# Squares of the first two blocks moved inside SBUF, and their scaling placed two output products earlier, in a fused attention and MLP kernel

## The chip, the cores and the metric

The kernel runs on one core of one Trainium2 chip. The metric is device time in microseconds (us), the median of three runs: 485.56 us (485.5 to 487.13).

The engines are named as in the profile: PE is TensorE's matrix multiplication and PEld its weight loads, DVE is VectorE, ACT is ScalarE, POOL is GpSimd and SP is SyncE, which here only issues DMA transfers. DMA transfers are issued by SP or by POOL, each in the order in which its instructions were written.

## The reference

```python
def _A_ref(x, wqkv, wo):                       # linear attention, 32 heads of 16
    q, k, v = ...                              # from x @ wqkv
    phi = lambda t: where(t > 0, t + 1, exp(t)) + 1e-6
    pq, pk = phi(q), phi(k)
    kv = einsum("bhsd,bhse->bhde", pk, v)
    z = einsum("bhsd->bhd", pk)
    num = einsum("bhqd,bhde->bhqe", pq, kv)
    den = einsum("bhqd,bhd->bhq", pq, z)[..., None] + 1e-6
    return (num / den) @ wo

def _B_ref(x, w1, b1, w2):                     # Dense, Mish, Dense
    h = x @ w1 + b1
    return (h * tanh(softplus(h))) @ w2

mod = (silu(c) @ w_mod).reshape(1, 6, 1, -1)   # sa, ca, ga, sb, cb, gb
h = layernorm(x) * (1 + ca) + sa
x = x + ga * _A_ref(h, wqkv, wo)
h = layernorm(x) * (1 + cb) + sb
x = x + gb * _B_ref(h, w1, b1, w2)
```

x is 2048 x 512, wqkv 512 x 1536, wo 512 x 512, w1 512 x 1792 and w2 1792 x 512, all in float32.

## The kernel before, in words

**Tiles.** The 2048 rows are four blocks of 512 rows, a block is four tiles of 128 rows. Most SBUF tiles are 128 x 512 float32 (2 KB in each partition) and come from one pool of `SLOTS` = 95 equal slots (tag "T"); a new tile takes a slot that an earlier one has given back. Each operand of a product is split into an upper part (rounded to fp32r, on ACT, line 82) and the rest (on DVE, line 88), and a product is three matmuls (lines 72 to 76). Part of the MLP's products are done by a Strassen-like scheme with seven products of sums in place of eight (`product`, line 1189).

**Order.** The order on each engine is the order in which the program issues its instructions (`manual_schedule`). Side work is written as Python generators: `spawn` queues one, and `tick` (line 57) lets every running one issue its next piece. So a statement "one tick later" says where in each engine's order the instructions stand. An engine that waits for an operand holds up all that stands behind it.

**The stage around the change.** After the query products, the loop of line 1338 issues the attention output products `o_unit` of blocks 1 to 3, counted by n = 4 b + t from 4 to 15; `o_unit` is twelve matmuls on PE (line 938). Beside it run, by ticks:

- `attend(3)` (line 878), spawned at n = 5. For block 3 it forms the denominators, sends their reciprocals to DRAM (line 890) and loads them spread over the partitions in four transfers `rd` (line 894), both on SP. After three ticks it multiplies the query tiles by them (DVE, line 902), two at the tick of n = 9 and two at that of n = 10. The splits follow: `qs_..h` on ACT, `qs_..l` on DVE one tick later. The product of n = 12, block 3's first, is the first that needs them.
- `norm_first(b, t)` (line 951) for blocks 0 and 1. It normalizes the finished rows (ACT, line 208) and turns each tile in 32 x 32 squares into a wide tile (DVE, line 239; the tag "W" has a single buffer). After a block's fourth tile the squares go to DRAM, `spread` on SP (line 245, four transfers of 256 KB, each from 32 partitions). Then four transfers bring them back (line 252, SP) as tiles with features along the partitions. For block 0 this last step is two ticks later (`WAIT = (2, 0)`), at n = 7.
- `turned_f(b, j)` (line 1025) scales such a tile on ACT (line 256, `hf_n`). The dictionary `turn_at` (line 1337) sets when. Block 0 is scaled at n = 10 (tiles 0 and 2) and n = 11 (tiles 1 and 3), each followed by a `split_b`. Block 1 is scaled at n = 13.

**Behind it.** At n = 13 `pairs_begin` (line 1208) starts the MLP's first products with block 0's split tiles (b11). `columns_early(0)` (line 1046) then makes the sums t1 to t4 of blocks 0 and 1 on DVE (line 1054) and splits them. `two_pairs` (line 1272) runs the products of the first two pairs with them; for them it calls `pair_first` of the second pair (a12 times b21) ahead of everything else. Its last step but one is the first product with w2 (`d_unit`, lines 74 to 76, tile `oacc`), which needs the split of w2's first tile. `w2_job` (line 707) makes that; `WAITS` (line 1382) says after how many ticks each of the first three starts.

**Late in the kernel** `load_r` (line 1418) loads rows of block 2 or 3 into a tile of its own tag "Y" (4 KB in each partition, one buffer).

Of the kernel before, what the change touches and what calls it, by code (L numbers as in the profile page):

```python
# [8 lines left out]
F32 = mybir.dt.float32  # L9
# [4 lines left out]
P = 128  # L14
# [3 lines left out]
NB = S // 512  # L18
NF = F // P
LAG = 3  # L20
SLOTS = 95
EPS = 1e-5
TINY = 1e-6

# [1 line left out]
def block_kernel(ctx: ExitStack, tc: tile.TileContext, x, wqkv, wo, w1, b1t, w2, c, wmodt, out):  # L26
    nc = tc.nc
    act, dve, pool, pe, sp = nc.scalar, nc.vector, nc.gpsimd, nc.tensor, nc.sync

    cst = ctx.enter_context(tc.tile_pool(name="cst", bufs=1))  # L30
    big = ctx.enter_context(tc.tile_pool(name="big", bufs=1))
# [6 lines left out]
    def sb(name, dt=F32, shape=(P, 512)):  # L38

        return big.tile(list(shape), dt, tag="T", name=name, bufs=SLOTS)  # L40

# [8 lines left out]
    def spawn(gen):  # L50
        fresh.append(iter(gen))
# [58 lines left out]
    c0 = sb("c0")  # L110
# [73 lines left out]
    def ln_stats(key, b, j, t):  # L184

        for d, name, shape in (mv, "mv", [P, 4, 2]), (rs, "rs", [P, 4]), (nb, "nb", [P, 4]):
            if (key, b) not in d:
                d[key, b] = cst.tile(shape, F32, tag=name, name=f"{name}_{key}_{b}", bufs=NB)
        st6 = cst.tile([P, 6], F32, tag="st6", name=f"st6_{key}_{b}_{j}", bufs=4)
        dve.bn_stats(st6, t)  # L190
        dve.bn_aggr(mv[key, b][:, j, :], st6)
# [4 lines left out]
    def ln_rstd(key, b, lo=0, hi=4):  # L196

        y = rs[key, b][:, lo:hi]
        pool.tensor_tensor(y, y, half[:, lo:hi], op=ALU.pow)  # L199
# [33 lines left out]
    wide, squares, turned = {}, {}, {}  # L233
# [7 lines left out]
    def spread(key, b, eng=sp):  # L241
        d = drp.tile([16, 32, 4, P], F32, name=f"sq_{key}_{b}")
        w = wide.pop((key, b))
        for a in range(4):
            eng.dma_start(bass.AP(tensor=d.tensor, offset=d.offset + P * a, ap=[[D, 32], [32 * D, 16], [1, P]]),
                          w[32 * a:32 * (a + 1)].rearrange("p m t c -> p m (t c)"))
        squares[key, b] = d

    def load_squares(key, b, j, eng=sp):
        d = squares[key, b]  # L250
        v = turned[key, b, j] = sb(f"sq_{key}_{b}_{j}")
        eng.dma_start(v, bass.AP(tensor=d.tensor, offset=d.offset + P * D * j, ap=[[D, P], [1, D]]))
# [689 lines left out]
    def later_sums(b, t):  # L942

        s_, v = first_sums.pop((b, t)), xt["r", b, t]
        if ("n", b) not in rs:
            for d, name in (rs, "rs"), (nb, "nb"):
                d["n", b] = cst.tile([P, 4], F32, tag=name, name=f"{name}_n_{b}", bufs=NB)
        act.activation(sb(f"scrap_n_{b}_{t}"), v, AF.Square, scale=-1.0 * D, bias=s_[:, 0:1], accum_out=s_[:, 1:2])
        return s_

    def norm_first(b, t):

        if (b, t) in SEEDED:
            if b:
                yield
            s_ = later_sums(b, t)
            yield
            dve.tensor_scalar(rs["n", b][:, t:t + 1], s_[:, 1:2], 1.0 / D ** 3, EPS, op0=ALU.mult, op1=ALU.add)
            ln_rstd("n", b, t, t + 1)
            yield  # L960
            dve.scalar_tensor_tensor(nb["n", b][:, t:t + 1], s_[:, 0:1], -1.0 / D, rs["n", b][:, t:t + 1],
                                     op0=ALU.mult, op1=ALU.mult)
        elif b and t > 1:
            ln_stats("n", b, t, xt["r", b, t])
            ln_eps("n", b, t, t + 1)
            ln_rstd("n", b, t, t + 1)
            yield
            ln_shift("n", b, t, t + 1)
        else:
            if b:  # L970
                yield
            sums = act_sums("n", b, t, xt["r", b, t])
            yield
            sums_eps("n", b, t, sums)
            yield
            sums_shift("n", b, t, sums)
        v = sb(f"n_{b}_{t}")
        ln_apply("n", b, t, xt["r", b, t], v, act)
        yield
        turn("n", b, t, v)  # L980
        if t == 3:
            yield
            spread("n", b)
            for _ in range(WAIT[b]):
                yield
            for j in (0, 2, 1, 3):
                load_squares("n", b, j)

    SEEDED = [(0, 0), (0, 1), (0, 2), (0, 3), (1, 0), (1, 1)]
    SEEDS = [(0, 0), (0, 1), (0, 2), (0, 3), (), (), (1, 0), (1, 1)]  # L990
# [4 lines left out]
            if i:  # L995
                o_seed(*i)

    WAIT = (2, 0)

    def norm_tile(b, t):  # L1000

# [27 lines left out]
    def split_b(b, j, name):  # L1029
        return split(f"{name}_{b}_{j}", hf[b, j], op_b, (name, j % 2))  # L1030
# [15 lines left out]
    def columns_early(c0):  # L1046

        b11, b12, b21, b22 = [[hf.pop((b, c + h)) for c in range(2)] for h in (0, 2) for b in (c0, c0 + 1)]
        t = [[sb(f"t_{c0}_{c}_{i}") for i in range(4)] for c in range(2)]
        todo = {}  # L1050

        def diff(c, i):
            u, v = ((b12[c], b11[c]), (b22[c], t[c][0]), (b22[c], b12[c]), (b21[c], t[c][1]))[i]
            dve.tensor_tensor(t[c][i], u, v, op=ALU.subtract)

        def upper(name, c, v):
            todo[name, c] = split(f"{name}_{c0}_{c}", v, op_b, (name, c))
            next(todo[name, c])

        for c in range(2):  # L1060
            diff(c, 0)
            diff(c, 1)
            upper("t2", c, t[c][1])
        for c in range(2):
            upper("t1", c, t[c][0])
        yield
        for name in "t2", "t1":
            for c in range(2):
                run(todo[name, c])
        for c in range(2):  # L1070
            diff(c, 2)
            upper("t3", c, t[c][2])
        yield
        for c in range(2):
            run(todo["t3", c])
            diff(c, 3)
        yield
        for name, v in ("t4", [t[c][3] for c in range(2)]), ("b22", b22):
            for c in range(2):
                upper(name, c, v[c])  # L1080
        yield
        for name in "t4", "b22":
            for c in range(2):
                run(todo[name, c])
# [145 lines left out]
    def pair_first(c0, g, p11):  # L1230
        m = mish(product(g, "a12", "b21", onto=p11), c0, 2 * g)
        next(m)
        spawn(m)
# [37 lines left out]

    def two_pairs(c0, g0, g1, begun, between):

        if c0 == 0:
            pair_first(c0, g1, begun[1][1])
        s0 = pair_early(c0, g0, begun[0], "h")
        tick()
        pc = product(g1, "s1", "t1", "h")
        pair_middle(g0, *s0)
        tick()  # L1280
        pa, p11 = begun[1]
        if c0:
            pair_first(c0, g1, p11)
        u2 = sb(f"u2_{g1}")
        product(g1, "s2", "t2", onto=pa)
        act.activation(u2, pa, AF.Copy)
        tick()
        pair_end(c0, g0, *s0, step=False)
        between[0]()
        pair_middle(g1, pa, pc, u2)  # L1290
        tick()
        between[1]()
        tick()
        pair_end(c0, g1, pa, pc, u2)
# [39 lines left out]
            load_wb(6)  # L1334


    turn_at = {10: [(0, 0), (0, 2)], 11: [(0, 1), (0, 3)], 13: [(1, 0), (1, 2), (1, 1), (1, 3)]}
    for b in range(1, NB):
        for t in range(4):
            n = 4 * b + t  # L1340
            if n == 13:
                begun = pairs_begin(("h", "tp"))
            for i, j in turn_at.get(n, ()):
                turned_f(i, j)
                if not i:
                    spawn(split_b(i, j, f"b{j // 2 + 1}1"))
            seed_next()
            if t == 3 and b == NB - 1:
                spawn(rows(2, 3))
            o_unit(b, t)  # L1350
            if n == 13:
                spawn(columns_early(0))
            if b == 1:
                spawn(norm_first(1, t))
            if n == 11:
                for f in range(4):
                    load_w2(f)
            if n == 5:
                spawn(attend(3, 3, sp))
            tick()  # L1360
# [18 lines left out]
            yield  # L1379
        yield from gen  # L1380

    WAITS = {0: 1, 1: 2, 2: 2}
    JOBS = {1: (0, 1, 2), 2: (3, 4), 3: (5, 6), 4: (7, 8), 5: (9, 10), 6: (11, 12, 13)}
    for g in range(1, G):
        for f in JOBS[g]:
            spawn(after(WAITS.get(f, 0), w2_job(f)))
        if g + 1 < G:
# [21 lines left out]
    banks, rq, U = {}, {}, {}  # L1409
# [8 lines left out]

    def load_r(n, c):

        y = rq[n, c] = big.tile([P, 16, 64], F32, tag="Y", name=f"rq_{n}_{c}", bufs=1)
        for a, d in enumerate(in_squares(x1d[L + n], c)):
            sp.dma_start(y[32 * a:32 * (a + 1)], d)

# [39 lines left out]
    rn, V, Z = {}, {}, []  # L1464
# [63 lines left out]
    for n, g in enumerate(pairs):  # L1528
# [20 lines left out]
        if n == 0:  # L1549
            begun = [pair_begin(L, pairs[i], ("tp" if i else "h", "acc")) for i in range(2)]  # L1550
# [16 lines left out]
    for k, (name, n) in enumerate(units[:4 * G]):  # L1567
        for _ in range(2 if k in (6, 10, 14, 18) else 1):
            if ahead_of:
                nm, m = ahead_of.pop(0)  # L1570
                spawn(left_prep(nm, pairs[m]))
        for _ in range(2 if k < 3 else 1):
            if loads:
                nm, m = loads.pop(0)
# [14 lines left out]
    for t in range(4):  # L1589
        p = last[t][:, 0:D // 2]  # L1590
# [3 lines left out]
        v = rn[t // 2][:, t % 2, :]  # L1594
# [35 lines left out]
```

## Time and profile before

| what | before |
|---|---|
| median of three runs | 485.56 us (485.5 to 487.13) |
| the profiled execution | 488.12 us, span 486.4 us |
| granted TensorE clock, mean | 0.995 |
| PE busy | 478.1 us, 98% |
| DVE busy | 393.9 us, 81% |
| ACT busy | 309.4 us, 64% |
| POOL busy | 119.8 us, 25% |
| DMA | 89.10 MB, mean 183 GB/s |
| HBM read and written | 59.52 MB and 27.00 MB |

The span goes from the first to the last instruction of one profiled execution; the execution is 1.72 us longer than that. A row of the timeline gives start and length in us, engine, source line, operation, output tile <- input tiles, how many it stands for, and in brackets how long the engine had been idle before it and whose result ended that. The times are from the start of the span. "SPq" is SP's queue of DMA issues; such a row shows how long the issue took, not the transfer. Rows that stand for several instructions ("x2") give the time from the first's start to the last's end. The view by stages gives the busy time (and the number of instructions) of PE, PEld, DVE, ACT and POOL in a stretch, then the granted TensorE clock, the share of the 16 DMA engines' time in use, and GB/s.

### The profile page before, as it was taken

The page shows a single profiled execution, that of the slowest core. Times are in us where ns is not written, and L with a number is a line of the kernel's source. Part 1 is how long each engine was busy: PE and PEld are TensorE (multiplying, and loading weights), DVE is VectorE, ACT ScalarE, POOL GpSimd, SP SyncE. Part 2 cuts the span into 40 slices and gives each one's busy share as a digit, 9 for nine tenths or more (in the row PEclk, how much of TensorE's full clock was granted, in tenths as well). Part 3 has the DMA queues.
Part 4 walks back from the last instruction along what each step waited for, and adds up shares of the span by engine and source line. Part 5 has one row for each costly group of instructions (what it writes and reads, how often), then busy time and mean ns, then how long its engine had stood idle before and what let it go on. Part 6 is the DMA issues. An engine that isn't in the chain of part 4 may idle for free.

```text
span 486.4 us, 7005 instructions
## 1 busy us (share of the span) xinstructions
PE 478.1 (98%) x2290; PEld 390.3 (80%) x2290; DVE 393.9 (81%) x785; ACT 309.4 (64%) x555; POOL 119.8 (25%) x200
## 2 busy tenths in 40 slices
PE   8999999999999997999999999999999999999997
PEld 7688877768887886787888888888888888888887
DVE  6899898998899797699689883699635687779992
ACT  5886468756666974778777765695265677547600
POOL 3673121000022211102223524343111101354400
PEclk9999999999999999899999999999999999999999
DMA  8904859543865349868439849989553502486964
GB/s 301 385 7 89 193 113 282 178 141 109 261 186 130 103 108 259 266 206 238 144 97 276 262 126 280 395 286 314 153 156 87 119 12 86 109 216 157 233 160 102
DMA packets 86399, 89.10 MB, mean 183 GB/s; under 512 B 22961, under 2 KB 59321, under 8 KB 86362
## 3 DMA queue, kind: packets, MB, share of 16 engines
q1 hardware_dynamic: 61320, 53.37, 36.9%
q0 software_dynamic: 22784, 34.49, 25.9%
q10 hardware_dynamic: 2258, 0.79, 0.7%
q8 instruction: 18, 0.29, 0.2%
q14 instruction: 19, 0.16, 0.1%
HBM read 59.52 MB, written 27.00 MB: 178 GB/s over the span
## 4 chain that ended last, share of the span: by engine, by line
PE 73%; DVE 9%; DMA 8%; ACT 5%; issue 2%; SPq 1%; POOL 1%; DVEq 0%
PE p_a L1195 14%; PE p_s L1195 7%; PE oacc L75 5%; PE oacc L76 5%; PE oacc L74 5%; PE m L76 5%; PE m L74 5%; PE m L75 5%; PE p L1195 3%; DMA sq_x<-wide_x 2%; PE pq_a L376 2%; PE o L938 2%; PE gacc L75 1%; PE pq L74 1%; DMA rd<-rden_d 1%
## 5 line engine op out<-in xcount | busy, mean ns | idle before, releaser
L1200 DVE TENSOR_TENSOR cb<-p_s,u 128x512 f32<-128x512 f32 x28 | 19.2, 688 | 10.7 <-ACT u L1248 10.7
L777 POOL DMA_DIRECT2D wb<-w2d x14 | 9.8, 705 | 64.6 <-issue 23.5
L1187 ACT ACTIVATE ub<-cb,b1c 128x512 f32<-128x512 f32 x28 | 20.0, 718 | 7.0 <-DVE cb L1200 6.8
L199 POOL TENSOR_TENSOR rs_n<-rs_n,half 128x1 f32<-128x1 f32 x16 | 9.7, 608 | 45.5 <-DVE rs_n L225 19.8
L1526 POOL DMA_DIRECT2D wt_m<-w2t x20 | 14.0, 702 | 25.3 <-DVE cb L1200 12.4
L1205 ACT ACTIVATE p<-p_a 128x512 f32<-128x512 f32 x12 | 7.0, 582 | 20.6 <-PE p_a L1195 12.2
L1162 ACT ACTIVATE u<-p,b1c 128x512 f32<-128x512 f32 x14 | 9.6, 686 | 13.3 <-PE p L1195 13.3
L1248 ACT ACTIVATE u<-p_a 128x512 f32<-128x512 f32 x14 | 8.4, 598 | 14.1 <-PE p_a L1195 13.9
L890 POOL DMA_DIRECT2D rden_d<-rden x2 | 1.5, 736 | 60.0 <-DVE rden L888 60.0
L256 ACT ACTIVATE hf_n<-sq_n,mc 128x512 f32<-128x512 f32 x16 | 12.3, 806 | 5.6 <-DMA sq_n<-sq_n 5.4
L1162 ACT ACTIVATE u<-p_a,b1c 128x512 f32<-128x512 f32 x14 | 9.6, 686 | 8.6 <-PE p_a L1195 8.5
L783 POOL DMA_DIRECT2D w2b<-w2d x20 | 10.6, 542 | 15.5 <-PE oacc L76 6.1
L290 DVE SCALAR_TENSOR_TENSOR ku<-e_k,relu_k 128x512 f32<-128x512 f32 x16 | 11.0, 685 | 2.0 <-ACT relu_k L288 2.0
L902 DVE SCALAR_TENSOR_TENSOR q<-q,rd 128x512 f32<-128x512 f32 x16 | 10.5, 685 | 1.7 <-DMA rd<-rden_d 1.7
L290 DVE SCALAR_TENSOR_TENSOR q<-e_q,relu_q 128x512 f32<-128x512 f32 x16 | 10.7, 690 | 1.4 <-ACT relu_q L288 1.4
L199 POOL TENSOR_TENSOR rs_x<-rs_x,half 128x1 f32<-128x1 f32 (+1 forms) x10 | 7.8, 785 | 15.7 <-DVE rs_x L194 14.9
L190 DVE BATCH_NORM_STATS2 st_x<-x 128x6 f32<-128x512 f32 x13 | 8.8, 677 | 2.9 <-DMA x<-in_x_dram 2.9
L287 ACT ACTIVATE e_k<-pk 128x512 f32<-128x512 f32 x16 | 9.5, 591 | 2.6 <-PE pk L76 2.6
L929 POOL DMA_DIRECT2D x1d<-r x8 | 4.4, 547 | 27.2 <-DVE r L924 27.2
L299 POOL DMA_DIRECT2D ku<-ku x8 | 7.2, 940 | 13.8 <-DVE ku L290 13.8
L175 DVE SCALAR_TENSOR_TENSOR wm<-wm,sc_row 128x512 f32<-128x512 f32 x16 | 10.5, 687 | 0.0
L716 DVE TENSOR_TENSOR w2g<-w2r,gb_bc 128x256 f32<-128x256 f32 x28 | 10.0, 420 | 0.0
(1611 smaller groups left out, 1883.5 us busy)
## 6 DMA issues: line engine op xcount, KB each, us to landing
wm<-in_wmodt_dram SPq DMA_DIRECT2D x24, 256.0 KB, 4.4
w1p<-in_w_dram SPq DMA_DIRECT2D x24, 256.0 KB, 6.4
w2b<-w2d POOLq DMA_DIRECT2D x20, 256.0 KB, 6.8
wt_m<-w2t POOLq DMA_DIRECT2D x20, 256.0 KB, 3.6
r<-in_x_dram SPq DMA_DIRECT2D x16, 256.0 KB, 3.0
sq_n<-wide_n SPq DMA_DIRECT2D x16, 256.0 KB, 3.7
sq_n<-sq_n SPq DMA_DIRECT2D x16, 256.0 KB, 6.7
x<-in_x_dram SPq DMA_DIRECT2D x15, 256.0 KB, 4.9
```

The lines of the kernel that those rows point to most:

```text
L74: pe.matmul(o, st[0], mv[0], start=start, stop=False)
L75: pe.matmul(o, st[0], mv[1], start=False, stop=False)
L76: pe.matmul(o, st[1], mv[0], start=False, stop=stop)
L199: pool.tensor_tensor(y, y, half[:, lo:hi], op=ALU.pow)
L256: act.activation(dst.rearrange("p (t a i) -> p t a i", t=4, a=4), turned.pop((key, b, j)).rearrange("p (a t i) -> p t a i", a=4, t=4), AF. ...
L290: dve.scalar_tensor_tensor(dst, e, 1.0, r, op0=ALU.min, op1=ALU.add)
L783: pool.dma_start(w2s[f][i], w2d[f // 2, i][:, f % 2, :])
L1162: act.activation(u, p, AF.Mish, bias=b1c[:, f:f + 1])
L1187: act.activation(u, p, AF.Mish, bias=b1c[:, f:f + 1])
L1195: pe.matmul(p, st, mv, start=onto is None and c == 0 and i == 0, stop=c == 1 and i == 2, skip_group_check=onto is not None)
L1200: dve.tensor_tensor(out, p, u, op=ALU.add)
L1526: pool.dma_start(v, w2t[g][:, :, SUM[name], :])
```

## The change

It has five parts.

1. `move_squares` replaces `spread` and `load_squares` for blocks 0 and 1. The wide tile goes straight into a second SBUF tile `V` (8 KB in each partition, one buffer, used by both blocks in turn) in 16 transfers of 64 KB, each from 32 partitions to 32 partitions, 512 bytes at a time. They are issued alternately by SP and POOL, at the place where `spread` stood. The two ticks of wait for block 0 are dropped.
2. The scaling of block 0 is issued at n = 8 and n = 9 in place of 10 and 11. Its four splits are issued at n = 11, behind that product.
3. In `two_pairs` the second pair's first product is issued at its later place (behind the first pair's third sum product) for the first call too.
4. `WAITS`: the first `w2_job` starts without a wait (1 tick before), the third after 3 ticks (2 before).
5. The slots of tag "T" are 93 in place of 95, and `load_r` uses half of a tile of tag "V" in place of "Y".

```diff
-SLOTS = 95
+SLOTS = 93
@@
+    def move_squares(key, b, queues):
+
+        w = wide.pop((key, b))
+        v = big.tile([P, 4, 4, P], F32, tag="V", name=f"sq_{key}_{b}", bufs=1)
+        n = 0
+        for a in range(4):
+            for m in range(4):
+                queues[n % len(queues)].dma_start(
+                    v[32 * m:32 * (m + 1), :, a, :],
+                    w[32 * a:32 * (a + 1), m:16:4].rearrange("p j t c -> p j (t c)"))
+                n += 1
+        for j in range(4):
+            turned[key, b, j] = v[:, j].rearrange("p a i -> p (a i)")
@@ in norm_first, after the fourth tile
-            spread("n", b)
-            for _ in range(WAIT[b]):
-                yield
-            for j in (0, 2, 1, 3):
-                load_squares("n", b, j)
+            move_squares("n", b, QUEUES[b])
@@
-    WAIT = (2, 0)
+    QUEUES = (sp, pool), (sp, pool)
@@ two_pairs
-        if c0 == 0:
-            pair_first(c0, g1, begun[1][1])
         s0 = pair_early(c0, g0, begun[0], "h")
         tick()
         pc = product(g1, "s1", "t1", "h")
         pair_middle(g0, *s0)
         tick()
         pa, p11 = begun[1]
-        if c0:
-            pair_first(c0, g1, p11)
+        pair_first(c0, g1, p11)
@@
-    turn_at = {10: [(0, 0), (0, 2)], 11: [(0, 1), (0, 3)], 13: [(1, 0), (1, 2), (1, 1), (1, 3)]}
+    turn_at = {8: [(0, 0), (0, 2)], 9: [(0, 1), (0, 3)], 13: [(1, 0), (1, 2), (1, 1), (1, 3)]}
@@ the loop of n
             for i, j in turn_at.get(n, ()):
                 turned_f(i, j)
-                if not i:
-                    spawn(split_b(i, j, f"b{j // 2 + 1}1"))
...
             if n == 13:
                 spawn(columns_early(0))
+            for j in {11: (0, 2, 1, 3)}.get(n, ()):
+                spawn(split_b(0, j, f"b{j // 2 + 1}1"))
@@
-    WAITS = {0: 1, 1: 2, 2: 2}
+    WAITS = {1: 2, 2: 3}
@@ load_r
-        y = rq[n, c] = big.tile([P, 16, 64], F32, tag="Y", name=f"rq_{n}_{c}", bufs=1)
+        y = rq[n, c] = big.tile([P, 2, 16, 64], F32, tag="V", name=f"rq_{n}_{c}", bufs=1)[:, 0]
```

## The prediction

> **What bounds the kernel now.** I read the busy times first, then who waits for whom on PE, then the timeline around PE's longest wait, engine by engine.
>
> ```profile
> PE 478.1 (98%) x2290; PEld 390.3 (80%) x2290; DVE 393.9 (81%) x785; ACT 309.4 (64%) x555; POOL 119.8 (25%) x200
> PE o L938 <- ACT qs_2h L82: 2.4, 1, 2.4
> ```
>
> PE bounds the kernel, and it has one long wait, 2.4 us for ACT. Only time given back to PE can shorten the run. Next PE around that wait, then two stages with the granted clock (the number ahead of the DMA share).
>
> ```profile
> 190.49 0.39 PE L938 MATMUL o<-m_0h,qs_0h 128*128 128x512 f32 x1
> 191.63 0.39 PE L938 MATMUL o<-m_1h,qs_1l 128*128 128x512 f32 x1
> 194.45 0.50 PE L938 MATMUL o<-m_2h,qs_2h 128*128 128x512 f32 x1 [2.44 <-ACT qs_2h L82]
> 200.39 0.39 PE L938 MATMUL o<-m_0h,qs_0h 128*128 128x512 f32 x1
> ...
> 194.00:196.00 2.00, 1.55 (x4) 1.02 (x5) 1.57 (x3) 2.00 (x5) 0.00 (x0) 0.72 1.09 318
> 196.00:198.00 2.00, 2.00 (x6) 1.52 (x6) 1.60 (x4) 2.00 (x4) 0.17 (x1) 0.50 0.42 142
> ```
>
> The first two rows are five matmuls apart, 0.227 us from start to start. Between 190.49 and 200.39 stand 24 matmuls (the product of n = 12 and the twelve of `pairs_begin`), 5.44 us of work that took 9.90. **The stall costs 4.46 us**: 2.59 of standing still (the next matmul was due at 191.86, came at 194.45), and 1.87 because the clock then fell to 0.72 and 0.50. Now ACT, DVE and SP's queue before it.
>
> ```profile
> 181.07 1.52 ACT L208 ACTIVATE n<-r,nb_n,rs_n 128x512 f32<-128x512 f32 x2 [2.92 <-DVE nb_n L961]
> 183.75 1.52 ACT L208 ACTIVATE n<-r,nb_n,rs_n 128x512 f32<-128x512 f32 x2 [1.15 <-DVE nb_n L961]
> 192.36 1.52 ACT L256 ACTIVATE hf_n<-sq_n,mc 128x512 f32<-128x512 f32 x2 [3.92 <-DMA sq_n<-sq_n]
> 193.79 0.61 ACT L82 ACTIVATE qs_2h<-q 128x512 fp32r<-128x512 f32 x1
> ...
> 184.90 0.69 DVE L239 STREAM_TRANSPOSE wide_n<-n 128x512 f32<-128x512 f32 x1
> 187.08 0.69 DVE L902 SCALAR_TENSOR_TENSOR q<-q,rd 128x512 f32<-128x512 f32 x1 [0.92 <-DMA rd<-rden_d]
> 191.13 0.69 DVE L902 SCALAR_TENSOR_TENSOR q<-q,rd 128x512 f32<-128x512 f32 x1 [0.36 <-DMA rd<-rden_d]
> 191.74 0.68 DVE L924 TENSOR_TENSOR r<-o,r 128x512 f32<-128x512 f32 x1
> ...
> 170.71 3.13 SPq L245 DMA_DIRECT2D sq_n<-wide_n  x4
> 178.12 0.58 SPq L890 DMA_DIRECT2D rden_d<-rden  x1
> 180.68 2.57 SPq L894 DMA_DIRECT2D rd<-rden_d  x4
> 183.42 1.98 SPq L252 DMA_DIRECT2D sq_n<-sq_n  x4
> ```
>
> ACT stood 3.92 us at block 0's first scaling, for squares that left at 170.71 and were fetched back from 183.42 on, behind the four `rd` transfers. `qs_2h`, which PE needs, is queued behind that scaling. Its input (DVE's row 191.13) was done at 191.82, so only the scaling held it. The fetch of 1 MB also shared SP's queue with `rd`, for which DVE waited 0.92 and 0.36 us.
>
> **The change, part by part.** First the rows that price the new transfers.
>
> ```profile
> L890 POOL DMA_DIRECT2D rden_d<-rden x2: 704/736/767, 132.6 to 144.9; - x2
> L890 SPq DMA_DIRECT2D rden_d<-rden x2: 580/630/679, 161.4 to 178.1; - x2
> L299 POOL DMA_DIRECT2D ku<-ku x8 | 7.2, 940 | 13.8 <-DVE ku L290 13.8
> DMA to landing us min/median/max: 2.7/3.7/4.5
> DMA to landing us min/median/max: 3.6/5.1/7.0
> ...
> 174.00:176.00 2.00, 2.00 (x14) 1.62 (x10) 1.72 (x3) 2.00 (x6) 0.00 (x0) 1.00 0.96 231
> 176.00:178.00 2.00, 2.00 (x10) 1.68 (x9) 1.97 (x5) 1.84 (x5) 0.55 (x1) 1.00 0.21 51
> ```
>
> *The 16 transfers.* No row shows one from SBUF to SBUF. The nearest is `rden_d`: 64 KB in pieces of 512 bytes too, 0.63 us of issue on SP and 0.736 on POOL. SP's eight take 5.0 us, POOL's eight 5.9. The first landing row is that of the wide tile's transfers (also from 32 partitions), the second that of `rd`. Value taken: POOL's 5.9 plus 3.7 = **9.6 us** from the last turned square to the last landing. Lower bound: 5.0 plus 2.7 = 7.7. Upper: POOL at the 0.94 of its dearest issue, 7.5, plus 7.0 = 14.5. I stay near the low end because the last two rows show 1 MB from 32 partitions at a time, sent from 170.71 on, gone by about 176: the share falls from 0.96 to 0.21.
>
> *Block 0.* The squares are ready at 170.7, so they land at 180.3 (178.4 to 185.2). SP is free again at 175.7, ahead of `rden_d` at 178.12, so `attend(3)` is not held up there. POOL is free at 176.6; its next work is block 1's `rs_n`, and the result of that is used at 181.
>
> *The scaling at n = 8 and 9.* On ACT it now stands between the two pairs of L208. The first pair ends at 182.59, 2.3 us after the landing: no wait. Two scalings take 1.43 us (192.36 to 193.79), so the second pair starts at 184.02 in place of 183.75 and its first result is there at 184.84, in time for DVE's turn at 184.90. The other two scalings end near 187.0; `qs_1h` behind them needs the product of DVE's row 187.08, there at 187.77 before. Cost on the path: nothing, covered by ACT's own idle time (1.15 us ahead of the second L208 pair, the rest behind it). From that turn to the end of row 191.74's step DVE has ten operations, 7.44 us (184.90 to 192.34, at 0.60 a step) of which 1.28 is waiting for `rd`. Without the fetch beside it I take `rd` as in time. `qs_2l` then runs from 191.06 to 191.7 and PE wants it at 192.31 (third matmul of its step): no stall, 0.6 us to spare. If `rd` still comes as late, 0.7 us of stall stays. So landing may be as late as 183.2, or **12.5 us** after the last turn, before PE notices.
>
> *The splits at n = 11.* Four on DVE behind the rest of `attend(3)`: the first ends at 193.5, PE's second matmul of `pairs_begin` is due at 193.44. I take 0.2 us of new stall for this, 0 to 0.7 with the case above.
>
> *Block 1 and what follows.* Its last turn comes at about 187.6 (was 188.39, DVE's waits gone), the landing at 197.2 (195.3 to 202.1). ACT reaches its scaling when `pairs_begin` and two copies are done, near 196.7. What follows hangs on it:
>
> ```profile
> 203.31 0.69 DVE L924 TENSOR_TENSOR r<-o,r 128x512 f32<-128x512 f32 x1 [3.48 <-PE o L938]
> 220.52 1.43 DVE L716 TENSOR_TENSOR w2g<-w2r,gb_bc 128x256 f32<-128x256 f32 x4
> 221.86 0.69 DVE L88 TENSOR_TENSOR w_0l<-w2g,w_0h 128x512 fp32r<-128x512 f32 x1
> 222.15 0.39 PE L74 MATMUL oacc<-w_0h,a_0h 128*128 128x512 f32 x1
> 222.60 0.50 PE L75 MATMUL oacc<-w_0l,a_0h 128*128 128x512 f32 x1
> ```
>
> Here lies the next wait. DVE worked almost without a break from 203.31 to 222.55, and PE stood 0.22 us at 222.60 for the last of it, `w_0l`. PE now comes 4.46 us sooner and wants `w_0l` at 217.92. DVE's row 203.31 waited for PE and moves with it. Then the reorder helps: `a_2l`, one step of 0.60, moves behind `w_0l`, since the second pair's first product is later, and the four `w2g` steps (1.34) do too, by `WAITS`. So `w_0l` comes 1.9 us earlier in DVE's order, and the 0.22 goes. That product's later place is 1.36 us on PE either way, no time by itself; it brings t1 to t3 nearer by as much, which DVE meets, by counting 0.60 a step, with over 2 us in hand. Counted the same way, the landing may slip to about 199.1, **11.5 us** after the turn; after that PE loses a microsecond for each.
>
> *Two slots fewer and the shared tag.* Eight tiles leave the pool just here, so pressure rises only later. The tightest reload of w2 I found:
>
> ```profile
> 326.12 2.16 POOL L783 DMA_DIRECT2D w2b<-w2d  x4
> 340.83 0.39 PE L74 MATMUL oacc<-w2b,a_7h 128*128 128x512 f32 x1
> DMA to landing us min/median/max: 3.6/6.8/9.4
> 340.00:400.00 60.00, 60.00 (x267) 49.67 (x266) 36.93 (x71) 31.85 (x55) 5.60 (x8) 1.00 0.41 108
> ```
>
> Its first pair is issued by 327.2 and lands by 336.6 at worst, 4.2 us ahead of use. Each step of twelve matmuls (2.72 us) gives back four slots, so two fewer mean some 1.4 us. Taken at nothing; 0 to 1.
>
> **Sum.** -4.46 - 0.22 + 0.2 = -4.5 us. The profiled execution, 488.12 us (span 486.4 and 1.72 around it), would come to 483.6. It is 2.56 us longer than the median of the runs, 485.56; I take the same loss off that: **481.1 us**.
>
> **The rivals.**
>
> *The transfers run one after another* (slower). If each of the 16 takes a quarter of the 3.7 us of a four times larger one, and they do not overlap, the landing comes 14.8 us after the turn. That is 2.3 us past the point of block 0 and 3.3 past that of block 1, and the clock falls once or twice as above: 5.6 + 1.87 to 3.74, against the 4.68 saved, 488.4 to 490.3, say **489.4**. It beats the gain from about 13.4 us on. For it: 32 partitions to 32 partitions. Against it: the fall of the DMA share at 176. [...]
>
> *Block 1's squares come 1 to 2 us past their point.* The stall moves to `two_pairs`; 1.5 us and perhaps the clock's 1.87: 482.6 to 484.5, say **483.6**. For it: SP's w2 loads now follow at once and share the DMA engines, and the upper bound is past the point. Against it: 1.9 us of room at the value taken. [...]
>
> *The gain is given back elsewhere*, to the smaller pool or to another order on DVE, which has no break in this stage: PE waits later for what it waited for here, about **485.3**. Against it: the stage of 340 to 400 above, where PE is busy for all of its 60 us, and PE's list of waits, in which the row shown is the longest.
>
> **How the numbers follow.** Forecast 0.61, squares of block 1 late 0.17, given back 0.12, one after another 0.10. A measurement of this kernel can tell about 0.5% from no change, 2.43 us: faster is below 483.1, slower above 488.0. Faster: 0.61 and half of the 0.17, 0.70; same: 0.20; slower: 0.10. The forecast's own range is 480.2 to 482.3 (the 0.2 at 0 to 0.7, a slot's 0 to 1, and 0.7 of spread). The full one reaches to 486.4, over the second and third case.
>
> **What would show it.** PE without the row at 194.45 and with clock 1.00 in all stages there; ACT's block 0 scalings between its L208 pairs with no wait for DMA; `rd` waits on DVE gone; block 1's scaling waiting at most 1 us; no wait before `w_0l`. Wrong if landing takes over 11.5 us, or if PE shows a new wait behind 200.

## The result, and the profile after

The changed kernel takes **483.67 us** (median of 6 runs, 482.8 to 484.17) against 485.56 us (485.49 to 487.13, 6 runs) for the kernel before: a ratio of 0.9952 with a 95% interval of 0.9937 to 0.9967. The saving is 0.48%, a little under the 0.5% that a measurement of this kernel can tell from no change, but the interval leaves out a ratio of 1, and a second measurement (`after_again`, below) gives the same ratio. The profiled execution took 483.39 us, span 481.6, with a granted clock of 1.0.

First the busy times of after. Lines from 249 on of the kernel before have moved by 14: `o` is line 952, `q` 916, `r` 938, `rd` 908, `hf_n` 270; line 256 is now the new transfers.

```profile
PE 474.2 (98%) x2290; PEld 387.6 (80%) x2290; DVE 393.5 (82%) x785; ACT 309.3 (64%) x555; POOL 128.9 (27%) x216
```

The top of PE's list of waits (in total, times, longest):

```profile
PE warm L136 <- POOL ones L130: 1.1, 1, 1.1
PE pk L604 <- DVE hT_x_0l L590: 0.8, 1, 0.8
```

PE has the same 2290 matmuls in 3.9 us less busy time (a stage at a lower clock counts as busy: six matmuls at 0.50 fill all 2.00 us from 196 to 198 before), and no wait for `qs_2h` any more. The two longest waits left stand in the start of the kernel. Next PE's timeline from the product of n = 12 on:

```profile
190.27 0.39 PE L952 MATMUL o<-m_0h,qs_0h 128*128 128x512 f32 x1
191.63 0.39 PE L952 MATMUL o<-m_2h,qs_2h 128*128 128x512 f32 x1
193.38 0.50 PE L75 MATMUL p_a<-b_0l,a_0h 128*128 128x512 f32 x1
196.01 0.39 PE L952 MATMUL o<-m_0h,qs_0h 128*128 128x512 f32 x1
217.77 0.39 PE L74 MATMUL oacc<-w_0h,a_0h 128*128 128x512 f32 x1
218.00 0.39 PE L75 MATMUL oacc<-w_0l,a_0h 128*128 128x512 f32 x1
235.23 0.39 PE L76 MATMUL oacc<-w_2h,a_2l 128*128 128x512 f32 x1
```

One stage of the view by stages, the one that had a clock of 0.72 before:

```profile
194.00:196.00 2.00, 2.00 (x10) 1.64 (x9) 1.74 (x3) 0.47 (x1) 0.00 (x0) 1.00 0.97 266
```

The product with `qs_2h` comes on time (191.63), the clock stays at 1.00, and `w_0l` is there when PE wants it (218.00 stands 0.23 behind 217.77). Only `b_0l` cost a little: its matmul is the 13th behind the one of 190.27, due at 193.22 at 0.227 us for each matmul, and starts at 193.38. From 190.27 to 196.01 PE needs 5.74 us, against 9.90 before and 5.44 without any loss.

The group of all 16 scalings on ACT, with the idle time ahead of them in the last column:

```profile
L270 ACT ACTIVATE hf_n<-sq_n,mc 128x512 f32<-128x512 f32 x16 | 12.0, 802 | 0.0
```

The timeline of ACT, DVE and the two queues, again after:

```profile
181.45 1.51 ACT L270 ACTIVATE hf_n<-sq_n,mc 128x512 f32<-128x512 f32 x2
183.28 1.52 ACT L208 ACTIVATE n<-r,nb_n,rs_n 128x512 f32<-128x512 f32 x2 [0.33 <-DVE nb_n L975]
184.71 1.51 ACT L270 ACTIVATE hf_n<-sq_n,mc 128x512 f32<-128x512 f32 x2
196.82 2.94 ACT L270 ACTIVATE hf_n<-sq_n,mc 128x512 f32<-128x512 f32 x4
186.03 0.69 DVE L916 SCALAR_TENSOR_TENSOR q<-q,rd 128x512 f32<-128x512 f32 x1 [0.33 <-DMA rd<-rden_d]
...
168.91 0.71 DVE L239 STREAM_TRANSPOSE wide_n<-n 128x512 f32<-128x512 f32 x1 [0.38 <-ACT n L208]
169.65 5.89 SPq L256 DMA_DIRECT2D sq_n<-wide_n  x8
169.93 4.40 POOL L256 DMA_DIRECT2D sq_n<-wide_n  x8 [4.69 <-DVE wide_n L239]
177.06 0.59 SPq L904 DMA_DIRECT2D rden_d<-rden  x1
179.59 2.64 SPq L908 DMA_DIRECT2D rd<-rden_d  x4
187.42 5.52 SPq L256 DMA_DIRECT2D sq_n<-wide_n  x8
```

The view of line 256 (ns of issue: shortest, median, longest; then from issue to landing in us, which the profile has for the transfers issued by POOL alone), and one microsecond of the view by stages:

```profile
L256 SPq DMA_DIRECT2D sq_n<-wide_n x16: 595/624/918, 169.7 to 192.1; - x16
L256 POOL DMA_DIRECT2D sq_n<-wide_n x16: 548/551/597, 169.9 to 191.7; - x16
DMA to landing us min/median/max: 2.1/2.6/3.1
177.00:178.00 1.00, 1.00 (x6) 0.83 (x5) 0.97 (x3) 0.09 (x2) 0.00 (x0) 1.00 0.00 0
```

ACT waited 0.0 us for squares in this execution. Block 0's scaling stands on both sides of the second pair of line 208, as the prediction placed it. Block 0's last turn ends at 169.62, SP issues its last transfer by 175.54, and in the microsecond from 177 the DMA engines move nothing (share 0.00). So all 16 transfers are through by 177.0, 7.4 us after the turn at most.

### The profile page after: what moved, and what is told of

The parts are those of the page before. It is cut to its first block, busy times and chain, and to the rows that moved or that the text cites. A ratio compares the mean times of both kernels' runs of the same rounds, so it can differ in the third digit from the quotient of the medians.

```text
span 481.6 us, 7044 instructions
## 1 busy us (share of the span) xinstructions
PE 474.2 (98%) x2290; PEld 387.6 (80%) x2290; DVE 393.5 (82%) x785; ACT 309.3 (64%) x555; POOL 128.9 (27%) x216
## 4 chain that ended last, share of the span: by engine, by line
PE 85%; DVE 7%; DMA 3%; ACT 2%; issue 1%; POOL 1%; SPq 0%; DVEq 0%; ACTq 0%
PE p_a L1205 15%; PE o L952 9%; PE p_s L1205 8%; PE oacc L75 5%; PE oacc L76 5%; PE oacc L74 5%; PE m L75 5%; PE m L74 5%; PE m L76 5%; PE p L1205 4%; PE pq_a L390 2%; PE pq L74 2%; DMA sq_x<-wide_x 2%; PE pq L75 2%; PE pq L76 2%; PE pk L76 1%
## 5 line engine op out<-in xcount | busy, mean ns | idle before, releaser
L256 POOL DMA_DIRECT2D sq_n<-wide_n x16 | 8.7, 554 | 7.2 <-DVE wide_n L239 4.7
```

## The experiments

There are twelve runs (nine edited kernels, and the two of the comparison again), in three groups of four that each ran on one chip with the kernel before beside them. The medians of before in these groups are 485.8, 485.72 and 485.6 us.

For the readings I use one number from each trace: the time from the first matmul of n = 12 to the 197th behind it, the `oacc<-w_2h,a_2l` of 235.23 above. The shortest is that of `splits_sooner`, 190.18 to 234.84 = 44.66 us, which is 197 times 0.2267 us, so I take it that PE lost nothing in it. What a trace has above 44.66 is its loss in this stage. The rows of the kernel before and of `splits_sooner`:

```profile
239.97 0.39 PE L76 MATMUL oacc<-w_2h,a_2l 128*128 128x512 f32 x1
```

```profile
190.18 0.39 PE L952 MATMUL o<-m_0h,qs_0h 128*128 128x512 f32 x1
234.84 0.39 PE L76 MATMUL oacc<-w_2h,a_2l 128*128 128x512 f32 x1
```

| kernel | median us (runs) | ratio to before, 95% | profiled execution us | loss in the stage us | difference |
|---|---|---|---|---|---|
| before, first profile | 485.56 (6) | 1 | 488.12 | 4.81 | 483.31 |
| before_again | 485.81 (12) | 0.9997 [0.9982, 1.0013] | 487.52 | 4.25 | 483.27 |
| before_third | 485.91 (1) | | 485.91 | 3.23 | 482.68 |
| later_by_dram | 485.75 (12) | 1.0003 [0.9987, 1.0019] | 485.90 | 2.63 | 483.27 |
| fewer_slots | 486.02 (12) | 1.0004 [0.9985, 1.0024] | 486.91 | 3.77 | 483.14 |
| after, first profile | 483.67 (6) | 0.9952 [0.9937, 0.9967] | 483.39 | 0.30 | 483.09 |
| after_again | 483.4 (9) | 0.9952 [0.9932, 0.9972] | 482.95 | 0.53 | 482.42 |
| old_products | 483.7 (6) | 0.9960 [0.9946, 0.9974] | 483.68 | 0.72 | 482.96 |
| splits_sooner | 483.09 (10) | 0.9938 [0.9919, 0.9957] | 482.98 | 0.00 | 482.98 |
| early_by_dram | 486.6 (12) | 1.0016 [1.0001, 1.0032] | 485.17 | 2.41 | 482.76 |
| moves_sp | 486.53 (12) | 1.0010 [0.9990, 1.0030] | 486.37 | 3.32 | 483.05 |
| moves_only | 489.93 (6) | 1.0080 [1.0058, 1.0103] | 489.12 | 6.36 | 482.76 |
| moves_two_buffers | 488.41 (11) | 1.0055 [1.0035, 1.0074] | 486.98 | 0.60 | 486.38 |
| after_89_slots | 487.12 (12) | 1.0039 [1.0017, 1.0061] | 488.51 | 0.91 | 487.60 |

The last column is the profiled time less the loss. In the twelve profiled executions with 93 or 95 slots it is 482.4 to 483.3, whatever the kernel: to within 0.9 us, all that tells them apart lies in this one stage.

### The two kernels again: before_again, after_again, before_third

These are the same two kernels, with no edit.

> The kernel before, unchanged, for the spread of its own executions. In the changed kernel's trace the stage from n = 12 to the end runs 4.5 us shorter than in the trace of before, yet the medians differ by only 1.9 us. Theory A (the profiled execution of before was a long one): the wait for qs_2h is there in every execution, about 2.6 us, but the clock falls behind it only in some; most executions have a mean clock of 0.998 to 1.000 and a span near 483.8, and a profile with clock 0.995 is 2 to 3 us longer. Theory B (the gain is lost in the changed kernel): executions of before mostly have clock 0.995 and spans near 486, and the changed kernel's are near 482 with something else outside the span. Theory C: the wait itself is much shorter in most executions, below 1 us.

> The changed kernel, unchanged, beside the kernel before on one chip. All theories: 483 to 484.2 us, clock 0.999 to 1.000. Theory A expects its spread to be small (under 1.5 us) and a ratio of 0.994 to 0.997 again, because no wait is left in which the clock can fall.

> The kernel before once more, for the wait itself. Theory A (the wait for block 0's scaling varies with the landing of its squares, and the clock's fall that the first profile of before shows is rare): the profiled execution shows a granted clock of 1.00 in all stages, PE loses 1.5 to 3.5 us to waits between the product of n = 12 and the start of `two_pairs`, in one wait of 1 to 2.5 us or in several, and the span is 483 to 485. Theory B (the wait of 2.4 us with the fall of the clock is what every execution has, and the saving was lost elsewhere): the row of 2.4 us at `qs_2h` comes again with 0.5 to 0.7 of clock behind it, and the span is near 486.4.

The ratio of after is 0.9952 a second time. What the first profile of before had, though, is not what the kernel usually does. From the profile of `before_again` and then of `before_third`, ACT's first scaling of block 0 and PE's waits in the stage:

```profile
190.47 0.82 ACT L256 ACTIVATE hf_n<-sq_n,mc 128x512 f32<-128x512 f32 x1 [3.89 <-DMA sq_n<-sq_n]
193.07 0.50 PE L938 MATMUL o<-m_2h,qs_2h 128*128 128x512 f32 x1 [1.07 <-ACT qs_2h L82]
218.62 0.50 PE L1195 MATMUL p_s<-b_0h,s_0h 128*128 128x512 f32 x1 [0.47 <-DVE cb L1200]
```

```profile
189.09 1.75 ACT L256 ACTIVATE hf_n<-sq_n,mc 128x512 f32<-128x512 f32 x2 [2.85 <-DMA sq_n<-sq_n]
195.63 0.50 PE L75 MATMUL p_a<-b_1l,a_0h 128*128 128x512 f32 x1 [0.23 <-DVE b_1l L88]
217.00 0.50 PE L1195 MATMUL p_s<-b_0h,s_0h 128*128 128x512 f32 x1 [0.45 <-DVE cb L1200]
```

ACT waits for the squares each time, 2.85 to 3.92 us, and it starts at 189.09 to 192.36. At 192.36 (the first profile) PE waits 2.44 at `qs_2h` and its clock falls. When ACT can start at 190.47, PE waits 1.07 there and again at `cb`. At 189.09 PE's matmul with `qs_2h` is only 0.17 us late, and the time is lost further on. The loss is 3.2 to 4.8 us in these three, and the clock fell in one. Of the 94 executions of before in the three groups, 5 have a mean granted clock of 0.996 or less; the others have 0.999 or 1.0. (Where in the kernel the clock fell is on record for the profiled executions alone.) The profile of `before_again` is the longest of its 12 executions (487.52), so its row of waits is not typical either.

How late PE is at three places shows where the loss arises (start of a matmul, less the start of the first one of n = 12, less 0.2267 us for each matmul between):

| profile | at the first `qs_2h` | at the end of `pairs_begin` | at the end of the stage |
|---|---|---|---|
| before, first profile | 2.60 | 4.45 | 4.81 |
| before_again | 1.23 | 2.64 | 4.25 |
| fewer_slots | 0.90 | 2.30 | 3.77 |
| before_third | 0.17 | 1.60 | 3.23 |
| after, first profile | 0.00 | 0.30 | 0.30 |

So the loss of before is not one wait. With the clock at 1.00, some 1.4 us go between `qs_2h` and the end of `pairs_begin` (to waits such as the one for `b_1l`), and 1.5 to 1.6 us in `two_pairs`. In the first profile PE came later, and `two_pairs` cost it 0.36.

Theory A of `before_third` holds, and its rival (2.4 us and the clock's fall each time) does not. Of the theories for `before_again`, B (the gain is lost in the changed kernel) is out. A is right that the clock falls in few executions, and wrong that a wait of 2.6 us is in each; at `qs_2h` the two later profiles are nearer to C.

### The place of the wait: later_by_dram

This is the kernel before, with all four scalings of block 0 at n = 11, behind `qs_2h` and `qs_3h`.

```diff
-    turn_at = {10: [(0, 0), (0, 2)], 11: [(0, 1), (0, 3)], 13: ...}
+    turn_at = {11: [(0, 0), (0, 2), (0, 1), (0, 3)], 13: ...}
```

> The kernel before with DRAM transfers, but block 0's scaling issued at n = 11, behind qs_2h and qs_3h on ACT. If the position on ACT alone is the cause, PE's wait goes and the time is 483.5. If the landing of the squares (192.4 in the trace of before) is the cause, the wait moves: scaling, split and rest take 0.8, 0.6 and 0.7 us behind it, so pairs_begin, due at 193.2, waits some 2 to 3.5 us for b_0l, and the time is 485.5 to 487.

There is no difference: 485.75 us. The wait at `qs_2h` is gone, and PE now waits one product later:

```profile
193.81 0.51 PE L74 MATMUL p_a<-b_0h,a_0h 128*128 128x512 f32 x1 [0.56 <-ACT b_0h L82]
```

That the scaling stood ahead of `qs_2h` was not the price by itself: the squares came too late for the first MLP product as well. The wait moved as the second reading had it, but it is smaller than its 2 to 3.5 us: PE is 1.37 us late by the end of `pairs_begin`, and the other 1.26 of its loss lie in `two_pairs`.

### The transfers alone: moves_only, moves_two_buffers, after_89_slots

`moves_only` is the kernel before with parts 1 and 5 of the change (transfers, `V`, 93 slots), and the old scaling, order of products and `WAITS`. `moves_two_buffers` gives `V` a second buffer and pays for it with four slots. `after_89_slots` is the changed kernel with the same small pool.

```diff
-tag="V", ..., bufs=1)
+tag="V", ..., bufs=2)
-SLOTS = 93
+SLOTS = 89
```

> The new transfers with the old order: scaling of block 0 at n = 10 and 11 with its splits, two_pairs and WAITS as before. If the landing of the squares is what matters (my theory): they land near 178, ACT does not wait at n = 10, the 2.4 us wait of PE is gone, and only the 0.2 us wait for w_0l may come back: 483.5 to 484.2. If the earlier scaling is what does it (rival: the queue position on ACT), the wait stays in part, 485 or more.

> The new transfers with the old order of everything else, as in `moves_only`, but with two buffers for the squares in place of one (and 89 slots in place of 93). Theory A (in `moves_only` the time went because block 1's transfers had to wait until block 0's scaling at n = 11 gave back the one buffer, so that they left at 193.4 rather than at about 187.5): they leave at 187 to 188.5 here, ACT's scaling of block 1 has no wait of microseconds for them, the gaps of PE in `two_pairs` go, and the time is 483.5 to 485. Rival (the scaling at n = 10 and 11 itself costs, by what ACT has to do in front of pairs_begin): PE's gaps stay, 488 or more.

> The changed kernel with 89 slots in place of 93, and nothing else: the pool that `moves_two_buffers` had. Theory (what `moves_two_buffers` lost by its time came from the four slots that paid for the second buffer, as PE's gap of 2.9 us at 84 to 87 and of 1.1 at 153 in its trace show, and not from the old order of scaling): 486 to 488.5, with a gap of PE of over 1 us ahead of 190, and 0.3 to 0.7 us lost between 190 and 240 as in the profile of after. Rival (four slots cost nothing; the time of `moves_two_buffers` came from the old order in executions that its profile does not show): 483.2 to 484.2.

`moves_only` missed: the direct transfers alone make the kernel **4.1 us slower** (489.93 against 485.8). Its trace says why; SP's and POOL's transfers of block 1, ACT's scaling of it, and PE:

```profile
193.42 5.74 SPq L256 DMA_DIRECT2D sq_n<-wide_n  x8
193.69 4.34 POOL L256 DMA_DIRECT2D sq_n<-wide_n  x8 [7.92 <-ACT hf_n L270]
203.79 2.93 ACT L270 ACTIVATE hf_n<-sq_n,mc 128x512 f32<-128x512 f32 x4 [7.03 <-DMA x1d<-r]
215.36 0.50 PE L1205 MATMUL p_a<-t_0h,s_0h 128*128 128x512 f32 x1 [2.57 <-ACT u L1251]
```

`V` has one buffer. Block 1's transfers have to wait until block 0 is scaled, and at the old place that ends at about 193.4; POOL stood 7.92 us for it. They leave 6.0 us later than in after (193.42 against 187.42), and ACT's scaling of block 1 stands 7.03 us. (The releaser named there, `x1d`, is not its input; the squares are.) The wait at n = 12 is gone, ACT scales block 0 at 187.31 without a wait, and of the 6.36 us of loss 5.8 lie behind `pairs_begin`, with the largest wait in `two_pairs`. So the time lies in the range of the rival (485 or more), but neither theory had this mechanism.

With a second buffer this goes, as the theory said:

```profile
189.74 6.08 SPq L256 DMA_DIRECT2D sq_n<-wide_n  x8
199.62 2.94 ACT L270 ACTIVATE hf_n<-sq_n,mc 128x512 f32<-128x512 f32 x4 [0.47 <-DMA w2r<-in_w_dram]
```

This execution ran 2.4 us behind after at n = 12 (192.67 against 190.27), so 189.74 is the place expected, and the loss in the stage falls from 6.36 to 0.60. So with a buffer for each block the old place of the scaling costs little in this stage. The total of 488.41 is a miss nevertheless. It lies in the rival's range, though PE's gaps in `two_pairs` did not stay, and `after_89_slots` shows most of its cause: that kernel takes 487.12 with nothing changed but the slots. From its profile, PE and DVE there, and the stage behind (granted clock 0.50):

```profile
87.15 0.50 PE L76 MATMUL pk<-wk_2h,hT_x_2l 128*128 128x512 f32 x1 [2.72 <-DVE hT_x_2l L88]
86.41 0.69 DVE L88 TENSOR_TENSOR hT_x_2l<-hf_x,hT_x_2h 128x512 fp32r<-128x512 f32 x1 [2.72 <-DMA ku<-ku]
```

```profile
88.00:90.00 2.00, 2.00 (x6) 1.54 (x6) 1.97 (x6) 0.00 (x0) 0.00 (x0) 0.50 0.11 42
```

A split of DVE waits for a transfer of `ku`, which is no input of it; `hT_x_2l` needs a slot, and I read the row as the wait for the one that `ku` gives back. In after the same split runs without a wait. By their medians `moves_two_buffers` is still 1.3 us above `after_89_slots`. Part of this goes with the clock: 7 of its 11 executions have a mean clock of 0.997 or less (median 488.77), against 6 of 12 in `after_89_slots`. The other four have a median of 487.29, against 486.61 for the other six there, which leaves 0.7 us. The intervals of the two ratios overlap, and the trace taken shows no loss for this rest, so it stays open.

### The early scaling without the transfers: early_by_dram

This is the changed kernel, but with blocks 0 and 1 through DRAM, fetched right behind the spread.

```diff
-            move_squares("n", b, QUEUES[b])
+            spread("n", b)
+            for j in (0, 2, 1, 3):
+                load_squares("n", b, j)
```

> The changed kernel with its early scaling (n = 8 and 9), order of products and slots, but the squares through DRAM again, with the fetch of block 0 asked for right behind the spread at n = 5. Theory A (the way through DRAM is longer by some 3 to 6 us and takes SP's queue ahead of `rden_d`; early scaling alone wins part): block 0's squares land at 182 to 186, ACT waits for them at n = 8 by 1 to 4 us, `rden_d` and `rd` come 1 to 3 us later, block 1's squares land at 198 to 202: 484.2 to 486. Rival (the price of before lay only in the place of the fetch behind `rd`, so asking sooner is all that is needed): no wait at n = 12 and 483.3 to 483.9, as the changed kernel. Third (the scaling at n = 8 in front of ACT's second pair now waits, and with it the product of n = 10 on): 486.5 or more.

It takes 486.6 us, a ratio of 1.0016 [1.0001, 1.0032]: nothing is won, and the rival (asking sooner is all that is needed) is out. The time is the third theory's, past the range of Theory A, but its mechanism is not in the trace: ACT's scaling at n = 8 did not wait. The profiled execution (485.17) is one of the shorter of the twelve, so whether the longer ones wait there is not seen. SP's queue and the two waits of DVE in it:

```profile
176.22 1.77 SPq L266 DMA_DIRECT2D sq_n<-sq_n  x4
178.04 0.57 SPq L904 DMA_DIRECT2D rden_d<-rden  x1
181.92 2.51 SPq L908 DMA_DIRECT2D rd<-rden_d  x4
185.56 0.69 DVE L916 SCALAR_TENSOR_TENSOR q<-q,rd 128x512 f32<-128x512 f32 x1 [0.92 <-DMA rd<-rden_d]
187.55 0.69 DVE L916 SCALAR_TENSOR_TENSOR q<-q,rd 128x512 f32<-128x512 f32 x1 [1.30 <-DMA rd<-rden_d]
200.99 2.33 ACT L270 ACTIVATE hf_n<-sq_n,mc 128x512 f32<-128x512 f32 x3 [2.69 <-DMA sq_n<-sq_n]
```

What is seen is Theory A's other half. `rden_d` goes 0.98 us later than in after, behind the fetch, and `rd` follows 3.31 us behind its end (1.94 in after), so DVE waits 2.2 us in all (0.33 in after). Block 1's squares come late too.

### Two queues or one: moves_sp

```diff
-    QUEUES = (sp, pool), (sp, pool)
+    QUEUES = (sp,), (sp,)
```

> The changed kernel with all 16 transfers of a block on SP's queue. By the issue times of after (8 in 5.89 us, 0.62 to 0.74 each) the 16 take 10 to 11.8 us: block 0's leave SP at 179.7 to 181.4, `rden_d` goes 2.6 to 4.3 us later than at 177.06, the four `rd` behind it too, and DVE waits 2 to 4 us for `rd` at n = 10 and 11; block 1's land at about 200, a microsecond past their point. 485 to 488. Rival (issue is not what spaces them: transfers in one queue are followed by the engines one after another anyway, so two queues bring nothing): 483.4 to 483.9.

It takes 486.53 us: without the second queue all of the gain is gone, and the rival (two queues bring nothing) is out.

```profile
169.96 10.45 SPq L256 DMA_DIRECT2D sq_n<-wide_n  x16
180.51 0.59 SPq L904 DMA_DIRECT2D rden_d<-rden  x1
186.81 0.69 DVE L916 SCALAR_TENSOR_TENSOR q<-q,rd 128x512 f32<-128x512 f32 x1 [1.77 <-DMA rd<-rden_d]
188.93 0.69 DVE L916 SCALAR_TENSOR_TENSOR q<-q,rd 128x512 f32<-128x512 f32 x1 [1.43 <-DMA rd<-rden_d]
```

Sixteen issues take 10.45 us (0.65 each), `rden_d` goes 3.45 us later than in after and DVE waits 3.2 us for `rd`. A single `rden_d` of 64 KB takes 0.59 us on the same queue, so I read the 0.65 as the time to issue one, not as a wait for the transfer ahead.

### The other parts: old_products, fewer_slots, splits_sooner

`old_products` puts the second pair's first product and `WAITS` back; `fewer_slots` is the kernel before with 93 slots; `splits_sooner` is the changed kernel with block 0's first two splits at n = 10.

```diff
-    WAITS = {1: 2, 2: 3}
+    WAITS = {0: 1, 1: 2, 2: 2}
```

```diff
-            for j in {11: (0, 2, 1, 3)}.get(n, ()):
+            for j in {10: (0, 1), 11: (2, 3)}.get(n, ()):
```

> The changed kernel with the old order of the second pair's first product in `two_pairs` and the old WAITS (the four `w2g` steps earlier). If DVE's order counts as the prediction has it: `w_0l` stands 1.9 us later in DVE's order, against 1.5 us that it had in hand ahead of its matmul in the profile of after (215.84 + 0.69 against 217.8 + 0.2): a wait of 0.2 to 0.6 us there, 483.7 to 484.2. If the order has no effect: 483.4 to 483.7, no wait at `w_0l`.

> The kernel before with 93 slots in place of 95, and nothing else. The prediction took the two slots at nothing, 0 to 1 us. If right: 485.3 to 486.2, no new gap of PE ahead of 190. If the pool is as tight as four slots fewer may show: 486.5 or more, and the change's own gain is larger than its time tells.

> The changed kernel with block 0's first two splits one step sooner (n = 10), the other two where they were. In the profile of after `b_0l` costs PE 0.17 us at 193.38. If those 0.2 to 0.5 us are what is left in this stage: 483.0 to 483.5, no wait at `b_0l`. If the splits push `qs_2l` of n = 11, with 0.6 us to spare by the prediction, past its matmul: a wait of 0.2 to 0.8 us there and 483.5 to 484.3.

In `old_products` the wait for `w_0l` is back, as the count of DVE's order said, and in `splits_sooner` the one for `b_0l` is gone:

```profile
218.21 0.50 PE L75 MATMUL oacc<-w_0l,a_0h 128*128 128x512 f32 x1 [0.16 <-DVE w_0l L88]
```

```profile
193.13 0.39 PE L75 MATMUL p_a<-b_0l,a_0h 128*128 128x512 f32 x1
```

The first costs 0.32 us (0.55 from start to start in place of 0.23). The 483.7 of `old_products` lies on the border between its two readings, so the row decides: the order has an effect, too small for the medians. The 483.09 of `splits_sooner` lies in its first range. By their ratios neither is told apart from after. `splits_sooner` has the lowest median of all, is faster than before by its whole interval (0.9938, at most 0.9957) and has no loss left in this stage. `fewer_slots` shows no difference from before, and its loss lies in the same stage.

## Why the prediction was right and wrong

**What held is the sum made against the profiled execution.** It came to 483.6 us; the changed kernel's median is 483.67 and its profiled execution 483.39. Against the same instruction of the first profile of before, PE of after is 0.23 us ahead at n = 12 (as it has been since 113 us, so this is not the change's) and 4.74 ahead at 235.23; from there to the end it stays 4.74 to 4.75. So 4.51 us were won in this stage, -4.5 by the prediction: 4.81 of loss down to 0.30, with the new stall at `b_0l` that the prediction had at 0.2. This is not luck, since it did not hang on the execution that was profiled: any of the profiles of before, less its own loss, comes to 482.7 to 483.3.

**What failed is the step behind it: "I take the same loss off that", 485.56 to 481.1.** The profiled execution of before was 2.56 us above the median and 1.0 above the highest of the three runs, and the prediction never asked what made it so. The loss itself did: less its loss in the stage, that execution is like the others (483.31 in the table). The median of 94 executions of before, 485.73, is about 2.7 us above the table's middle of 483.0. If the rest takes as long in the executions without a profile, a usual one loses about 2.7 us here, not 4.8. After has 483.4 to 483.67, some 0.4 to 0.7 us above. The gain on the median is the 1.9 and 2.4 us measured. The excess of the profile belonged to the term that the change removes; the sum should have ended at 483.6. This lies above the forecast's own range (480.2 to 482.3) and inside the full one. The upper end of the own range was also too low by its own terms: 0.5, 1 and 0.7 added to 481.1, as the lower end adds them, give 483.3. The prediction gave 0.70 to a time below 483.1; the measured one is above it.

**The clock's part of the stall, 1.87 us, was read too simply.** The clock of 0.72, 0.50 and 0.93 in the three stages from 194 to 200 takes 1.70 us from PE. But `before_again` and `before_third` lose 1.4 us between the same matmuls at a clock of 1.00. So it is not shown that without the fall this execution would have been 1.87 us shorter there; how much the fall added stays open. The sum is not touched by this, since the change removes these waits too.

**The transfers.** The issue times were off on both queues, in opposite ways: SP 5.89 us for eight (forecast 5.0), POOL 4.40 (5.9). The squares were there 7.4 us after the last turn at most, under the lower bound of 7.7 and well under the 9.6 taken. The rival of transfers one after another (14.8 us) is out: ACT scaled block 0 at 181.45, 11.8 us after the turn, without a wait. The second queue is worth 3 us (486.53 against 483.4 to 483.67): SP takes 10.45 us for all 16 against 5.89 for its eight, and `rden_d` stands behind them. What the second queue saves over `moves_sp` is time of issuing, and that is not small beside the transfer here: sixteen issues take 10.45 us, and one transfer has landed 2.6 us after its issue (median of those issued by POOL). It does not bring DMA engines of its own: SP's queue alone took 0.96 of the time of the 16 engines from 174 to 176 in before (the row is in the prediction), and POOL's alone 0.93 from 415 to 420 in after.

**`rd` in time.** It came 0.33 us late, against 1.28 in all before. PE's product of n = 12 was on time all the same, but DVE has no break from there to the split `b_0l`, done at 193.32 for a matmul due at 193.22. So this wait is behind the stall at `b_0l`: without it the split would have been done at 192.99. The forecast's 0.2 us of new stall counted this split at 193.5 with `rd` in time; that its size came out right is luck.

**The scaling at n = 8 and 9 "costs nothing".** This is true of ACT: the second pair of line 208 waited 0.33 us, with the cover as described. But the prediction saw only that cost and missed what the step gives. Block 0's last scaling ends at 186.2, 1.2 us before block 1's first transfer at 187.42 needs the one buffer. The prediction put 12.5 us of room on block 0's landing by what PE needs; this buffer is a nearer limit, and with the old scaling it makes `moves_only` 4.1 us slower than before.

**The order of the first product and `WAITS`.** This held: without them `w_0l` is late by 0.32 us in the trace, which the medians cannot tell.

**Two slots at nothing.** This held (1.0004 [0.9985, 1.0024]), but with little room: four more slots off the changed kernel cost 3.5 us, most of it by a wait at 84 to 87 (and by one of 0.72 us at 155), where the prediction had not looked. It had taken the reload of w2 at 326 as the tightest use.

**Block 1's squares late; gain given back elsewhere.** Neither came. The measured time is that of the first of these rivals (483.6), but not by its mechanism: ACT scaled block 1 at 196.82 without a wait, and PE's lead stays within 0.02 us from 240 to the end. The room is small, though: in `after_again` ACT waited 1.05 us at this place, and PE lost nothing by it.

## What to carry to other kernels

If the profiled execution is longer than every timed run, find out first which stage holds the excess. If it is the stage that the change clears, the sum ends at the profiled time less the whole stall; taking the stall off the median takes off an excess that the median does not have. A shorter path into a buffer of its own is worth nothing until that buffer is free in time: here the direct transfers alone made the kernel 0.8% slower, the early scaling alone brought nothing (0.2% slower), and both together made it 0.5% faster.

## What the hardware showed beside this

**The clock.** In the first profile of before PE stood 2.44 us and the clock then fell; in `after_89_slots` it stood 2.72 us, and the clock fell to 0.50 behind it. A wait of 2.52 us at the same place in `moves_two_buffers`, and the one of 2.57 us at 215.36 in `moves_only`, left it at 1.00. So behind a wait of 2.4 to 2.7 us the clock fell in two of these four executions. Of the 12 executions of `after_89_slots` six have a mean clock of 0.996 or less; their median is 488.25 us, that of the other six 486.61. A low clock goes with 1.6 us more there, near the 1.70 that the fall takes from PE in the first profile. Why the clock fell behind two of the four waits and not behind the other two, no run here shows.

**The queues.** For the same kind of 64 KB transfer inside SBUF, POOL issued in 0.551 us (median) and SP in 0.624, the reverse of their order for `rden_d` (0.736 and 0.630).
